# Turning q by DMA transposes of 16-bit halves instead of by TensorE, in a linear-attention and multiplicative-FFN kernel

## The chip, the cores and the metric

The kernel runs on one core of a Trainium2 chip. The metric is the time of one execution on the device, in microseconds; the time before is the median of three runs. The profile is one further execution of the same kernel, recorded by the hardware profiler.

The engines of the core are named as the profile names them: PE is TensorE (matmuls), PEld its weight loads, DVE is VectorE, ACT is ScalarE, POOL is GpSimd, and SP is SyncE, which issues most of the transfers. Each of them works through its own instructions in order, and waits for another engine where an instruction needs its result.

## What is computed

A linear attention without softmax, followed by a feed-forward part without a nonlinearity other than a product:

```python
# q, k, v: (8 batches, 8 heads, 576 tokens, 64), float32
kv  = np.einsum('bhsd,bhse->bhde', k, v)
out = np.einsum('bhsd,bhde->bhse', q, kv)
rms = np.sqrt(np.mean(out * out, axis=-1, keepdims=True) + 1e-06)
x   = out / rms * g_norm                      # then (B,H,S,D) -> (B*S, H*D): 4608 x 512
a   = x @ w1                                  # 512 -> 1024
b   = x @ w2                                  # 512 -> 1024
h   = a * b @ w3                              # 1024 -> 1024
return (h @ w_out).astype(np.float32)         # 1024 -> 512
```

The product of q with kv sums over the 64 dimensions of a head. A matmul on TensorE sums over partitions, so q must be turned: it comes from memory with tokens on the partitions, and the product wants dimensions on the partitions. This turning of q is what the change is about.

## The kernel before

The weights w3 and w_out are first multiplied together. Then the 4608 tokens are worked through in nine groups of 512: eight groups of the first 512 tokens of each batch, and one group of the eight batches' leftover 64 tokens each. All large matmuls use Strassen-Winograd's seven products. While the matmuls of a group run, the attention of the next batch is laid between them in eight pieces. The order on TensorE is as written; the order on the other engines is set by a scheduler outside the start-up.

One pair of heads of q (128 partitions x 512 words, 256 KB) is loaded into one of two buffers, turned by four transposes into a bank of PSUM, and copied to SBUF by ScalarE. The leftovers of two batches are turned together in the same way:

```python
def q_t(r):
    q_sb = loaded["q", b, r]
    qt_ps = bank(ps_at, "at").rearrange("p (e i t) -> p e i t", e=2, i=2)
    for e in range(2):
        for i in range(2):
            nc.tensor.transpose(qt_ps[:, e, i, :], q_sb[:, e, i * P:(i + 1) * P], ident)   # L297
    qT[r] = work.tile([P, 2, 2, P], FP32, name="qT")      # two buffers
    nc.scalar.copy(qT[r], qt_ps)                          # L299

def q_t_left():
    st["qT"] = work.tile([P, NP, P], FP32, name="qT_left", bufs=1)
    qt_ps = bank(ps_at, "at").rearrange("p (r t) -> p r t", r=NP)
    for r in range(NP):
        nc.tensor.transpose(qt_ps[:, r, :], q_left[b // 2][:, 2 * r:2 * r + 2, :], ident)  # L307
    nc.scalar.copy(st["qT"], qt_ps)                       # L308
```

The products that read the turned q, and the norm behind them:

```python
def product(h):                                           # heads of pairs 2h and 2h+1
    o_ps = [bank(ps_at, "at") for _ in range(2)]
    ...
        nc.tensor.matmul(o_ps[l][...], lhsT=qT[r][rows, e, i, tokens], rhs=kv_b[...], ...)  # L348
    return norm(o_ps, [...])     # squares (ScalarE), sums (VectorE), root (ScalarE), scale (VectorE)
```

How the attention is laid between the matmuls; piece n runs at the n-th call of `between`, which is called twice in each of the four Winograd blocks of a group:

```python
def begin_q(*rs):
    for r in rs:
        q_t(r)
        load_ahead("q", r)        # the load of the next q into the buffer that is now free

fs = [[] for _ in range(8)]
if b == 1:
    fs[0].append((a.begin_kv, 0, 1))
fs[0].append((a.begin_q, 0, 1))
fs[1] += [(a.begin_kv, 2, 3), (a.finish, 0)]              # finish(h): product(h) and its norm
fs[2].append((a.begin_q, 2, 3))
fs[3] += [(a.turn, 0), (a.turn, 1)]
if more:
    fs[5].append((batch(b + 1).begin_kv, 0, 1))
fs[5].append((a.finish, 1))
fs[7] += [(a.turn, 2), (a.turn, 3)]
if b % 2:
    fs[2].insert(0, (a.q_t_left,))
    fs[6].append((a.product_left,))
    fs[7].append((a.turn_left,))
    ...
```

One Winograd block, with the copies that ScalarE makes between the products. The matmul banks are a pool of five; a product into `r1` a second time adds to what stands in it, and so has to wait until ScalarE has copied it:

```python
def keep(name, ps):
    t = late_tile(name)...
    nc.scalar.copy(t, ps)                                 # L512
    return t

r1 = product("a11", "b11")                                # product: four matmuls, L499
p1 = keep("p1", r1)
r2 = product("s1", "t1")
p5 = keep("p5", r2)
product("s2", "t2", r1)
u2 = keep("u2", r1)
between()
product("s4", "b22", r2)
done("c12", r2, u2)
product("s3", "t3", r1)
u3 = keep("u3", r1)
done("c22", p5, u3)
r3 = product("a12", "b21")
done("c11", r3, p1)
between()
product("a22", "t4", r1)
done("c21", r1, None)                                     # copies half to c by ScalarE, L633
```

Of the kernel before, what the change touches and what calls it, by code (L numbers as in the profile page):

```python
# [10 lines left out]

FP32 = mybir.dt.float32
U32 = mybir.dt.uint32
I64 = mybir.dt.int64
AF = mybir.ActivationFunctionType
ALU = mybir.AluOpType
# [4 lines left out]
def kernel(  # L21
# [32 lines left out]
    nc = tc.nc  # L54
    PSUM = bass.MemoryType.PSUM
    P = 128
# [4 lines left out]
    NP = H // 2  # L61
# [11 lines left out]
    work = ctx.enter_context(tc.tile_pool(name="work", bufs=2))  # L73
    ps_mm = ctx.enter_context(tc.tile_pool(name="ps_mm", bufs=5, space=PSUM))
    ps_at = ctx.enter_context(tc.tile_pool(name="ps_at", bufs=3, space=PSUM))
# [5 lines left out]
    def bank(pool, tag):  # L81
        return pool.tile([P, 512], FP32, name=tag, tag=tag)


    loaded = {}
    q_left = {}
# [43 lines left out]
    def conversion(n, dst, raw, cols=slice(0, 1024)):  # L130

        dst, raw = (t if len(t.shape) == 3 else t[:, cols] for t in (dst, raw))
        if raw.dtype == FP32:
            yield
            nc.vector.tensor_copy(out=dst, in_=raw)
            return
        words = raw.bitcast(U32).rearrange("p (n w) -> p n w", w=2)
        lo, hi = words[:, :, 0], words[:, :, 1]

        low = ab[n % 2][:, NF // 2:].rearrange("p a i t -> p (a i t)")[:, cols]  # L140
        low_bits = low.bitcast(U32)
        if len(dst.shape) == 3:
# [96 lines left out]
    ident = const.tile([P, P], FP32, name="ident")  # L239
# [13 lines left out]
    def keep_warm(n):  # L253

        t = bank(ps_mm, "mm")
        for _ in range(n):
            nc.tensor.matmul(t[:, 0:P], lhsT=ident, rhs=ident, start=True, stop=True)


    def attention(b):  # L260
        kv_b = kv_sb[b % 3]
        qT = {}
# [35 lines left out]
            qT[r] = work.tile([P, 2, 2, P], FP32, name="qT")  # L298
            nc.scalar.copy(qT[r], qt_ps)  # L299

        st = {}

        def q_t_left():
            st["qT"] = work.tile([P, NP, P], FP32, name="qT_left", bufs=1)
            qt_ps = bank(ps_at, "at").rearrange("p (r t) -> p r t", r=NP)
            for r in range(NP):
                nc.tensor.transpose(qt_ps[:, r, :], q_left[b // 2][:, 2 * r:2 * r + 2, :], ident)  # L307
            nc.scalar.copy(st["qT"], qt_ps)  # L308

        def norm(o_ps, dsts):  # L310

# [98 lines left out]

        def begin_q(*rs):
            for r in rs:
                q_t(r)
                load_ahead("q", r)

        def begin(r):
            begin_kv(r)
            begin_q(r)

        def finish(h):  # L420
            all_of(product(h))

        return SimpleNamespace(**{f.__name__: f for f in (
            start, begin_kv, begin_q, begin, product, finish, turn, q_t_left, product_left, turn_left,
        )})

    batches = {}

    def batch(b):
        if b not in batches:  # L430
            batches[b] = attention(b)
        return batches[b]

    def steps(b):


        a = batch(b)
        a.start()
        more = b + 1 < B
        fs = [[] for _ in range(8)]  # L440
        if b == 1:
            fs[0].append((a.begin_kv, 0, 1))
        fs[0].append((a.begin_q, 0, 1))
        fs[1] += [(a.begin_kv, 2, 3), (a.finish, 0)]
        fs[2].append((a.begin_q, 2, 3))
        fs[3] += [(a.turn, 0), (a.turn, 1)]
        if more:
            fs[5].append((batch(b + 1).begin_kv, 0, 1))
        fs[5].append((a.finish, 1))
        fs[7] += [(a.turn, 2), (a.turn, 3)]  # L450
        if b % 2:
            fs[2].insert(0, (a.q_t_left,))
# [3 lines that stand above are left out]
                fs[7].append((load_q_left, b + 1))  # L456
        elif more:
            fs[0].append((load_q_left, b + 1))
        return iter([lambda s=s: [f(*args) for f, *args in s] for s in fs])
# [163 lines left out]
    def gates(T, p, between, ready=lambda name: None):  # L623
        def done(name, one, two):
            multiply(name, one, two)
            ready(name)

        def multiply(name, one, two):

            dst = ab[int(name[1]) - 1][:, p, int(name[2]) - 1, :]  # L630
            if two is None:
                c = late_pool.tile([P, N], FP32, name="c21")
                nc.scalar.copy(c, one[:, 0, :])  # L633
                nc.vector.tensor_mul(dst, c, one[:, 1, :])
# [245 lines left out]
    with tc.manual_schedule(  # L880
# [84 lines left out]
    groups = [*range(B - 1), B, B - 1]  # L965
    for n, T in enumerate(groups):
        pieces = steps(T + 1) if n + 2 < NG else iter([])

        def between():
            next(pieces, lambda: None)()  # L970

        for p in range(NF):
            if T and p + 1 == NF:
                sum_1, sum_2, sum_4, sum_3 = sum_ab(p)
                following = {
                    "c12": [], "c22": [sum_1],
                    "c11": [
                        lambda: sum_inner(0, lambda: all_of(f() for f in (sum_2, sum_3))),
                        lambda: sum_inner(1),
                    ],  # L980
                    "c21": [sum_4],
                }
                gates(T, p, between, lambda name: all_of(f() for f in following[name]))
                continue
            gates(T, p, between if T or p else lambda: None)
            if T == 0:
                if p + 1 < NF:
                    run(sum_w(p + 1))
                for _ in range(2):
                    if len(converted) < len(todo):  # L990
                        begin_next()
                        end_next()
                if p + 1 == NF:
                    allocate_projection()
                    run(*(f(i) for i in range(NF) for f in (sum_ab, combine_w3o)))
            else:
                run(sum_ab(p))
        last = n + 1 == NG
        if T:
            project_twice(T, last, [] if last else combine_x(groups[n + 1]))  # L1000
            continue
        project(T, between)
        run(combine_x(1))
        prepare_b()
        for _ in range(3):
            load_b()
        stage = stage_tile()
        inner_sums.append([stage[:, i] for i in range(3)])
# [30 lines left out]
```

## Time and profile before

| | |
|---|---|
| time, median of three runs | 794.01 us (793.12 to 795.03) |
| span of the profiled execution | 792.2 us |
| granted TensorE clock, mean | 0.999 of full speed |
| TensorE busy | 784.4 us, 99% |
| VectorE busy | 499.0 us, 63% |
| ScalarE busy | 282.2 us, 36% |
| DMA | 117.60 MB, mean 148 GB/s |
| transposes of q on TensorE | 128 of pairs (L297), 16 of leftovers (L307) |

A float32 matmul shows as two records, a transpose as one. The steady part of the kernel repeats every 79 to 80 us, once for each group of tokens: some 57 us of Winograd blocks with attention between them, then 22 us of the projection (L771). From 647 us on there is no attention left to lay between the matmuls. The first 100 us are the folding of w3 and w_out, the attention of batch 0 and the conversion of the weights; there, transfers are waited for.

### The profile page before, as it was taken

The page shows a single profiled execution, that of the slowest core. Times are in us where ns is not written, and L with a number is a line of the kernel's source. Part 1 is how long each engine was busy: PE and PEld are TensorE (multiplying, and loading weights), DVE is VectorE, ACT ScalarE, POOL GpSimd, SP SyncE. Part 2 cuts the span into 40 slices and gives each one's busy share as a digit, 9 for nine tenths or more (in the row PEclk, how much of TensorE's full clock was granted, in tenths as well). Part 3 has the DMA queues.
Part 4 walks back from the last instruction along what each step waited for, and adds up shares of the span by engine and source line. Part 5 has one row for each costly group of instructions (what it writes and reads, how often), then busy time and mean ns, then how long its engine had stood idle before and what let it go on. Part 6 is the DMA issues. An engine that isn't in the chain of part 4 may idle for free.

```text
span 792.2 us, 14634 instructions
## 1 busy us (share of the span) xinstructions
PE 784.4 (99%) x6003; PEld 683.1 (86%) x6003; DVE 499.0 (63%) x1050; ACT 282.2 (36%) x540; POOL 24.8 (3%) x36
## 2 busy tenths in 40 slices
PE   8999999999999999999999999999999999999998
PEld 5455788888899889988998899889988998899897
DVE  7968999425575558555755576457645765485366
ACT  6677643223332433233323332333233322222221
POOL 0010003410000000000000000000000000000000
PEclk9999999999999999999999999999999999999999
DMA  9996653574138412841284119411810180055015
GB/s 321 339 334 178 190 148 127 191 265 157 54 99 305 110 54 84 298 120 54 88 297 129 54 56 314 130 54 67 307 34 2 60 308 12 1 191 189 1 34 186
DMA packets 72582, 117.60 MB, mean 148 GB/s; under 512 B 16452, under 2 KB 60484, under 8 KB 72516
## 3 DMA queue, kind: packets, MB, share of 16 engines
q1 hardware_dynamic: 70064, 101.86, 40.2%
q10 hardware_dynamic: 2452, 14.81, 5.4%
q8 instruction: 47, 0.77, 0.4%
q14 instruction: 19, 0.16, 0.1%
HBM read 100.27 MB, written 16.38 MB: 147 GB/s over the span
## 4 chain that ended last, share of the span: by engine, by line
PE 96%; DMA 3%; ACT 1%; DVE 0%; SPq 0%; issue 0%; DVEq 0%; ACTq 0%
PE mm L499 58%; PE mm L771 22%; PE mm L481 6%; PE at L278 3%; PE at L348 2%; PE at L297 2%; PE at L381 2%; DMA raw<-in_moe_w_dram 2%; DMA raw<-in_moe_w_out_dram 1%; PE at L468 1%; PE mm L823 0%; PE at L366 0%; PE at L390 0%; PE at L307 0%; DVE inv L317 0%; ACT w_sb L149 0%
## 5 line engine op out<-in xcount | busy, mean ns | idle before, releaser
L499 PE MATMUL mm<-xT,w_sb 128*128 128x256 f32 x768 | 176.2, 379 | 0.0
L499 PEld LDWEIGHTS mm<-xT,w_sb 128*128 128x128 f32 x768 | 145.5, 190 | 20.0 <-issue 0.5
L499 PE MATMUL mm<-xc,ws 128*128 128x256 f32 x576 | 130.4, 379 | 0.0
L499 PEld LDWEIGHTS mm<-xc,ws 128*128 128x128 f32 x576 | 109.4, 190 | 15.2 <-ACT p L512 0.3
L637 DVE TENSOR_TENSOR c<-mm,u 128x512 f32<-128x512 f32 x36 | 24.9, 690 | 153.6 <-PE mm L499 153.4
L512 ACT COPY u<-mm 128x512 f32<-128x512 f32 x74 | 43.3, 585 | 146.5 <-PE mm L499 141.9
L512 ACT COPY p<-mm 128x512 f32<-128x512 f32 x74 | 43.3, 585 | 88.0 <-PE mm L499 85.5
L499 PE MATMUL mm<-xc,w_sb 128*128 128x256 f32 x288 | 69.6, 385 | 0.0
L771 PE MATMUL mm<-w3o_sb,raw 128*128 128x128 f32 x500 | 62.2, 275 | 0.0
L481 PE MATMUL mm<-chunks,ab 128*128 128x512 f32 x128 | 60.2, 601 | 1.6 <-ACT chunks L149 1.0
L499 PE MATMUL mm<-xT,ws 128*128 128x256 f32 x256 | 60.9, 381 | 0.4 <-ACT p L512 0.4
L771 PEld LDWEIGHTS mm<-w3o_sb,raw 128*128 128x128 f32 x500 | 59.0, 192 | 0.2
L499 PEld LDWEIGHTS mm<-xc,w_sb 128*128 128x128 f32 x288 | 52.5, 190 | 7.3 <-ACT u L512 0.3
L499 PEld LDWEIGHTS mm<-xT,ws 128*128 128x128 f32 x256 | 47.2, 190 | 6.7 <-ACT p L512 0.8
L638 DVE TENSOR_TENSOR ab<-c 128x256 f32<-128x256 f32 x108 | 46.7, 433 | 3.1
L637 DVE TENSOR_TENSOR c<-p,u 128x512 f32<-128x512 f32 x36 | 24.9, 691 | 35.5 <-ACT u L512 35.5
L771 PE MATMUL mm<-w3o_sb,ab 128*128 128x128 f32 x336 | 43.7, 275 | 0.0
L782 ACT COPY u<-mm 128x512 f32<-128x512 f32 x23 | 13.5, 585 | 83.9 <-DVE raw L795 43.4
L317 DVE TENSOR_REDUCE inv<-sq 128x8 f32<-128x512 f32 (+1 forms) x40 | 23.4, 627 | 31.6 <-ACT sq L316 31.6
L481 PEld LDWEIGHTS mm<-chunks,ab 128*128 128x128 f32 x128 | 21.9, 190 | 22.6 <-issue 15.8
L771 PEld LDWEIGHTS mm<-w3o_sb,ab 128*128 128x128 f32 x336 | 41.0, 192 | 0.3
L633 ACT COPY c<-mm 128x256 f32<-128x256 f32 x36 | 13.4, 372 | 48.4 <-PE mm L499 48.4
(150 smaller groups left out, 1109.9 us busy)
## 6 DMA issues: line engine op xcount, KB each, us to landing
w3o_sb<-w3o_l SPq DMA_DIRECT2D x26, 896.0 KB, 5.3
raw<-in_moe_w_dram SPq DMA_DIRECT2D x31, 512.0 KB, 7.4
raw<-w3o_l SPq DMA_DIRECT2D x13, 896.0 KB, 4.6
w3o_sb<-w3o_l ACTq DMA_DIRECT2D x11, 896.0 KB, 4.6
k_sb<-in_k_dram SPq DMA_DIRECT2D x32, 256.0 KB, 3.9
v_sb<-in_v_dram SPq DMA_DIRECT2D x32, 256.0 KB, 4.6
q_sb<-in_q_dram SPq DMA_DIRECT2D x32, 256.0 KB, 4.1
out_dram<-raw SPq DMA_DIRECT2D x14, 512.0 KB, 5.1
```

The source lines that it names most:

```text
L278: nc.tensor.matmul(kv_ps[e * D:(e + 1) * D, r - rs[0], :], lhsT=k_sb[:, e, cols] if j < J else kl[:, 2 * r + e, :], rhs=v_sb[:, e, cols] i ...
L297: nc.tensor.transpose(qt_ps[:, e, i, :], q_sb[:, e, i * P:(i + 1) * P], ident)
L317: nc.vector.tensor_reduce(out=inv[:, i], in_=sq.rearrange("p (h d) -> p h d", d=D), axis=AX.X, op=ALU.add)
L348: nc.tensor.matmul(o_ps[l][tokens, n * D:(n + 1) * D], lhsT=qT[r][rows, e, i, tokens], rhs=kv_b[rows, e, r, :], start=True, stop=True,)
L381: nc.tensor.transpose(t_ps[:, j, :], st[r // 2][:, j // 2, j % 2, m:m + 2, :], ident)
L481: nc.tensor.matmul(sums_ps[half][m], lhsT=w3T[half, c][:, m, :], rhs=chunks[:, c, 1, :], start=(c == 0), stop=(c == KF - 1),)
L499: nc.tensor.matmul(ps[:, u, :], lhsT=lhsT(a_name, u, c), rhs=rhs(b_name, c),  start=(u == 0 and c == 0 and to is None), stop=(c == chunks ...
L512: nc.scalar.copy(t, ps)
L637: nc.vector.tensor_add(c, one, two)
L638: nc.vector.tensor_mul(dst, c[:, 0, :], c[:, 1, :])
L771: nc.tensor.matmul(to[:, i, :], lhsT=x[:, c, :], rhs=y[:, c, :], start=new and place // 4 not in seen, stop=(c == 1), skip_group_check=True,)
L782: nc.scalar.copy(t[:, 0:4], ps[0])
```

## The change

Instead of transposing q on TensorE, the kernel uses the transpose that a DMA can do while it moves data within SBUF. [...] each float32 is taken as two 16-bit halves. ScalarE first copies q so that all first halves stand together and all second halves behind them (into the buffer that will hold the result); one DMA transposes all eight 128 x 128 blocks of halves back into the buffer of q; ScalarE puts the halves together again. The bits are not changed. Its purpose is to take the transposes of q off TensorE.

Batch 0, whose attention lies in the start-up, keeps the transposes on TensorE. Because the way by DMA is longer, pairs 0 and 1 of a batch are begun earlier: in piece 6 of the batch before, or, for batch 1, at the first piece of the first group.

```diff
+    def turn_by_dma(dst, src):
+        def words(t):
+            return t.bitcast(U16).rearrange("p (n w) -> p n w", w=2)
+        def planes(t):
+            return t.bitcast(U16).rearrange("p (w n) -> p w n", w=2)
+
+        nc.scalar.copy(planes(dst).rearrange("p w n -> p n w"), words(src))       # "split"
+        nc.sync.dma_start_transpose(
+            out=src.bitcast(U16).rearrange("p (a t) -> p a t", t=P), in_=dst.bitcast(U16)
+        )
+        nc.scalar.copy(words(dst), planes(src).rearrange("p w n -> p n w"))       # "merge"
 ...
+        def q_by_dma(r):
+            qT[r] = work.tile([P, 2, 2, P], FP32, name="qT")
+            turn_by_dma(
+                qT[r].rearrange("p e i t -> p (e i t)"), loaded["q", b, r].rearrange("p e n -> p (e n)")
+            )
 ...
         def q_t_left():
             st["qT"] = work.tile([P, NP, P], FP32, name="qT_left", bufs=1)
-            qt_ps = bank(ps_at, "at").rearrange("p (r t) -> p r t", r=NP)
-            for r in range(NP):
-                nc.tensor.transpose(qt_ps[:, r, :], q_left[b // 2][:, 2 * r:2 * r + 2, :], ident)
-            nc.scalar.copy(st["qT"], qt_ps)
+            turn_by_dma(
+                st["qT"].rearrange("p r t -> p (r t)"), q_left[b // 2].rearrange("p h d -> p (h d)")
+            )
 ...
         def begin_q(*rs):
             for r in rs:
-                q_t(r)
+                q_by_dma(r)
                 load_ahead("q", r)
 
         def begin(r):                      # batch 0 only
             begin_kv(r)
-            begin_q(r)
+            q_t(r)
+            load_ahead("q", r)
 ...
+        def begin_first():
+            if not first_done:
+                first_done.append(begin_q(0, 1))
 ...
-        fs[0].append((a.begin_q, 0, 1))
         fs[1] += [(a.begin_kv, 2, 3), (a.finish, 0)]
         fs[2].append((a.begin_q, 2, 3))
 ...
         fs[5].append((a.finish, 1))
+        if more:
+            fs[6].append((batch(b + 1).begin_q, 0, 1))
 ...
-            gates(T, p, between if T or p else lambda: None)
+            gates(T, p, between if T or p else lambda: batch(1).begin_first())
```

More of the change, by code (lines that the diff above doesn't have):

```diff
@@ L13 @@
 U32 = mybir.dt.uint32
+U16 = mybir.dt.uint16
 I64 = mybir.dt.int64
@@ L417, in begin @@
             begin_kv(r)
-            begin_q(r)
+            q_t(r)
+            load_ahead("q", r)
+        first_done = []
+        def begin_first():
+            if not first_done:
+                first_done.append(begin_q(0, 1))
         def finish(h):
@@ L423, in attention @@
         return SimpleNamespace(**{f.__name__: f for f in (
-            start, begin_kv, begin_q, begin, product, finish, turn, q_t_left, product_left, turn_left,
+            start, begin_kv, begin_q, begin_first, begin, product, finish, turn, q_t_left, product_left, turn_left,
         )})
```

## The prediction

> **What bounds the kernel now.** I read four views, in this order. First the page's busy times with the wait table of TensorE, to see which engine sets the end and whether it ever waits:
>
> ```profile
> PE 784.4 (99%) x6003; PEld 683.1 (86%) x6003; DVE 499.0 (63%) x1050; ACT 282.2 (36%) x540; POOL 24.8 (3%) x36
> ```
>
> ```profile
> PE mm L257 <- POOL ident masks.py:199: 2.0, 1, 2.0
> PE mm L481 <- ACT chunks L149: 1.0, 1, 1.0
> PE mm L481 <- ACT ab L473: 0.6, 1, 0.6
> PE mm L499 <- ACT p L512: 0.4, 1, 0.4
> ```
>
> TensorE is busy 99% of the span, and its own wait table (line waited for: us in total, times, longest) holds 4.0 us in all, half of it at the very start. So an instruction taken off TensorE shortens the span by what it takes there. The reader should not take busy time for that: matmul records overlap. The chain that ended last, in order of time, gives it without the overlap:
>
> ```profile
> 263.81 5.61 PE mm L499 x26
> 269.42 0.44 PE at L307 x4
> 269.86 0.87 PE at L297 x8
> 270.73 4.32 PE mm L499 x20
> ```
>
> Twelve transposes hold the chain for 0.44 + 0.87 = 1.31 us, or 0.109 us each, and the matmuls stand flush on both sides. The group table gives "17.2 us, 128 records" for L297, 0.134 us each; I use the chain.
>
> Third, ScalarE, because the change moves work there. It is 36% busy, but what counts is how late it may be. The timeline of a steady stage (one group of 512 tokens, 329 to 408 us):
>
> ```profile
> 346.45 3.62 PE L499 MATMUL mm<-xc,ws 128*128 128x256 f32 x16
> 346.65 0.58 ACT L512 COPY p<-mm 128x512 f32<-128x512 f32 x1 [1.15 <-PE mm L499]
> ...
> 348.37 0.58 ACT L512 COPY p<-mm 128x512 f32<-128x512 f32 x1 [1.14 <-PE mm L499]
> ...
> 349.90 1.04 PE L297 MATMUL at<-ident,q_sb 128*128 128x128 f32 x8
> 350.15 0.59 ACT L512 COPY u<-mm 128x512 f32<-128x512 f32 x1 [1.20 <-PE mm L499]
> ...
> 350.64 1.08 ACT L299 COPY qT<-at 128x512 f32<-128x512 f32 x2
> ```
>
> A Winograd product is 8 matmul records, 1.73 us. It is copied out of its bank while the next product runs, and the product after that accumulates into the same bank. So a copy of 0.58 us has 1.73 us less a start of about 0.2 us: ScalarE may be late by **about 0.95 us** before TensorE waits. The "1.15" idle time before each copy is the same margin seen from the other side. This is the number the case turns on.
>
> Fourth, the DMA issues: how long a transfer of this size takes to land.
>
> ```profile
> k_sb<-in_k_dram SPq DMA_DIRECT2D x32, 256.0 KB, 3.9
> ...
> q_sb<-in_q_dram SPq DMA_DIRECT2D x32, 256.0 KB, 4.1
> ...
> out_dram<-raw SPq DMA_DIRECT2D x3, 256.0 KB, 2.2
> ```
>
> **What the Trainium skill says.** "TensorE: Matmul & The Clock Gate", Part 4: PE-mode transpose, gives about 275 ns for a transpose in a kernel's context; the trace has 272 to 273 ns per record, but records overlap and each costs the engine 109 ns, so taking 275 would promise 35 us in place of 14. "ScalarE: Activation LUTs", What ACT_TABLE_LOAD costs, gives 0.833 ns per element beside a fixed part; the trace agrees (585 ns at 512 and 372 ns at 256 elements: 0.832 ns each). "VectorE: DVE Perf Modes", The three transpose paths, gives 1309 ns for one 128x128 transpose of 2-byte values by DMA. "DMA: Bandwidth & Descriptors", Latency and other measured facts, gives 261 GB/s for DMA transposes whose middle dimension is not contiguous. No transpose by DMA is in this trace, so the last two are estimates' raw material only.
>
> **The change part by part.** *Removed from TensorE.* Batches 1 to 7 lose 16 transposes each (112), and four leftovers of q lose 4 each (16). Batch 0 keeps its own. In the chain these are fourteen pieces of L297 after 100 us, thirteen of 0.87 and one of 1.03 us, and four of L307 at 0.44 us: 11.31 + 1.03 + 1.76 = **14.1 us**. That is the whole possible gain, 1.8% of 794.0, so a gain of over 2% is nearly excluded.
>
> *Moved on ScalarE.* Each of 32 turns (28 pairs of heads, 4 leftovers) loses one copy of 0.60 us (32 x 0.60 = 19 us) and gets two of 1024 16-bit elements, one that takes the halves apart and one that puts them together. 0.832 x 1024 and the fixed 0.16 us of the PSUM copies make 1.01 us; the conversions of 1024 elements out of SBUF (L149) took 1.17 us. I take 1.1 us: 64 x 1.1 = 70 us, net +51 us, ScalarE from 282 to about 333 us, 42%. No bound by itself.
>
> *Added on DMA.* 32 transposes of 256 KB within SBUF, 8.4 MB beside 117.6 MB. Bytes are no issue; the landing time is. Estimates: 256 KB at the skill's 261 GB/s is 1.0 us on top of the 2.2 us that a 256 KB store took here: 3.2 us at best. Eight blocks at 1309 ns one after another would be 10.5 us. I choose **4.0 us**, near the low end, since 16 engines should share the blocks, plus some waiting behind loads on the same queue.
>
> *The new wait.* ScalarE works in order. In the built kernel the order on ScalarE around the second product of a batch is
>
> ```
> split q2; squares x2; split q3; copy c; sqrt; copy p1; copy p5; merge q2; merge q3; copy u2
> ```
>
> and around the next batch's pairs
>
> ```
> split q0; squares x2; split q1; sqrt; copy c; merge q0; copy p1; merge q1; copy p5; copy u2
> ```
>
> A merge stands at the head of ScalarE until its transpose has landed, and the copies behind it free TensorE's banks. I lay these on the stage shown above.
>
> Group A (pairs 2, 3): the first product of the attention ends at about 342.9; split q2 343.0 to 344.1, squares to 345.2, split q3 to 346.3. SyncE issues loads of k and v until 345.1, so the first transpose lands at 345.1 + 4.0 = 349.1 and the second at about 350.6. Merges 349.1 to 350.2 and 350.6 to 351.7, then u2 to 352.3. With its transposes gone TensorE wants that bank at 349.90 + 1.73 = 351.6. Stall 0.7 us, seven times: 4.9 us.
>
> Group B (pairs 0, 1 of the next batch): split q0 ends at 372.65, its transpose lands at 376.65, merge to 377.75, p1 to 378.35, wanted at 376.7: stall 1.65 us. Merge q1 waits until 378.85, p5 is done at 380.55, wanted at 380.1 in batches without a leftover product: 0.45 us in half of them. 1.9 us on average, six times: 11.4 us.
>
> Leftovers: split and merge have one or two instructions between them, so ScalarE stands still for most of the landing time, at a place where the copies wanted next are a little later; I put 1.2 us on each of four, 4.8 us. The first group (batch 1, pairs 0, 1) lies in the start-up, where transfers are waited for anyway: 0.5 us.
>
> Sum: 794.0 - 14.1 + 4.9 + 11.4 + 4.8 + 0.5 = **801.5 us**.
>
> **The rivals.** *R1, the transfer is hidden.* If a transpose lands within about 3 us, group A fits in the margin, B loses a few tenths, and nearly all of the 14.1 us remains: 780 to 786 us. For it: the product that needs the turned q comes some 19 us after the split (269.9 to 288.8 in the stage before), DMA is busy 42% of the stage, ScalarE has idle time between all copies. Against it: the merges stand early in ScalarE's order, not just ahead of their use. *R2, the transpose is slow.* Every microsecond of landing beyond 4 is paid about 18 times (7 + 6 + 1 groups + 4 leftovers), since ScalarE's margin is spent by then. 6 us gives about 838 us; 10 us would give some 910. For it: 16-bit pieces, and the 1309 ns for one block. Against: the 261 GB/s. *R3, ScalarE becomes the bound by its work alone.* Two merges back to back are 2.2 us against a margin of 0.95; that would cost up to 1.2 us in each group A even at no landing time, but they follow a copy that has just been served, and the next one is not due for another 1.2 us. I give it under 5 us in all. *R4, SyncE's queue.* Loads of q now wait for merges, and loads of k and v stand behind them. Loads are issued a whole stage ahead, so I expect nothing from it outside the first 110 us.
>
> **How range and chances follow.** Landing times from 2.7 to 6 us span 782 to 838 us, and 4.0 lies at 801.5; break-even is near 3.5 us. Over 2% faster means under 778.1, below even a change with no cost (779.9): 0.03. Over 2% slower means over 809.9, a landing time of about 4.5 us: somewhat less likely than not, 0.37. The rest, 0.60, is within 2%.
>
> **What would show it.** Right: no L297 after 100 us on TensorE; ScalarE copies of 16-bit halves at 1.0 to 1.2 us, x64, busy about 333 us; transposes in the DMA issues landing in about 4 us; in the wait table of TensorE new lines of waits for ScalarE's p and u, about 20 us in all, and for ScalarE waits of merges on DMA. Wrong if those waits are near zero (R1), or far over 30 us (R2); also if the wait stands at the product that reads the turned q, which I expect never to wait, or at matmuls that want w or k and v (R4).

## The result, and the profile after

The changed kernel takes **918.17 us** (916.92 to 919.58), against 793.71 us for the kernel before (793.12 to 795.03): a ratio of **1.1566, 95% interval 1.1539 to 1.1593**. The prediction was 801.5 us with a range of 782 to 838. The direction of its sum was right, the size was not.

First the page's line of busy times:

```profile
PE 810.4 (89%) x5875; PEld 693.3 (76%) x5875; DVE 499.5 (55%) x1050; ACT 442.1 (48%) x572; POOL 27.5 (3%) x36
```

TensorE has 128 instructions fewer, as intended, and yet is busy 26 us longer. ScalarE is busy 442 us where the prediction had put 333. The groups of instructions say which of its instructions took the time (busy us, mean ns of one, idle time before and what ended it):

```profile
L270 ACT COPY qT<-q_sb 128x1024 uint16<-128x1024 uint16 x28 | 132.2, 4721 | 1.3 <-PE at L371 1.0
L274 ACT COPY qT<-q_sb 128x1024 uint16<-128x1024 uint16 x28 | 32.7, 1167 | 17.6 <-DMA q_sb<-qT 17.6
```

L270 is the split and L274 the merge. Both copy 1024 halves on 128 partitions. The merge takes 1.17 us, close to the 1.1 us that I took for both; **the split takes 4.72 us**. Nothing waits inside it: idle time before it is 1.3 us in all. The transfer between the two lands sooner than the 4.0 us that I chose (the DMA issues, median us from issue to landing):

```profile
q_sb<-qT SPq DMA_TRANSPOSE x28, 3.1
```

What a slow split does to TensorE stands in TensorE's wait table (us in total, times, longest):

```profile
PE mm L530 <- ACT p L543: 85.6, 13, 8.6
```

The wait is of the kind that the prediction described, a matmul that wants its bank back from ScalarE's copy of p, but thirteen times for 6.6 us on average. One of the thirteen, on the timeline of ScalarE (start, duration, what; in brackets the idle time before it):

```profile
405.29 4.74 ACT L270 COPY qT<-q_sb 128x1024 uint16<-128x1024 uint16 x1
410.05 1.09 ACT L339 ACTIVATE sq<-at 128x512 f32<-128x512 f32 x2
411.02 4.70 ACT L270 COPY qT<-q_sb 128x1024 uint16<-128x1024 uint16 x1
...
415.37 0.57 ACT L664 COPY c<-mm 128x256 f32<-128x256 f32 x1
415.83 1.08 ACT L543 COPY p<-mm 128x512 f32<-128x512 f32 x2
416.78 1.19 ACT L274 COPY qT<-q_sb 128x1024 uint16<-128x1024 uint16 x1
418.86 1.16 ACT L274 COPY qT<-q_sb 128x1024 uint16<-128x1024 uint16 x1 [0.89 <-DMA q_sb<-qT]
```

and the same moment on the timeline of TensorE:

```profile
406.99 1.89 PE L530 MATMUL mm<-xT,w_sb 128*128 128x256 f32 x8
408.71 1.89 PE L530 MATMUL mm<-xc,ws 128*128 128x256 f32 x8
416.48 3.78 PE L530 MATMUL mm<-xc,ws 128*128 128x256 f32 x8 [5.88 <-ACT p L543]
```

This is the order that the prediction had read from the built kernel (only the root and copy c have changed places): split, squares, split, root, copy c, copy p. The two splits fill 405.3 to 415.7. The product that ends near 408.9 is copied out only at 415.8. TensorE makes one more product, is done with it at 410.6, wants the first one's bank back, and stands for 5.88 us. The transfer is not what it waits for: the first merge comes behind that copy and finds its data there.

The last line shows one thing more. The eight records after the wait take 3.78 us, the eight before it 1.89 us. Three windows: before the end of that wait, after it, and the one that follows (length; busy time of PE, PEld, DVE, ACT, POOL with the number of instructions; granted TensorE clock; DMA share; GB/s):

```profile
410.00:416.40 6.40, 0.60 (x3) 0.19 (x1) 1.80 (x4) 6.38 (x8) 0.00 (x0) 0.93 0.24 44
416.40:422.40 6.00, 5.92 (x14) 4.76 (x15) 1.77 (x4) 3.32 (x5) 0.00 (x0) 0.51 0.53 131
422.40:426.40 4.00, 4.00 (x20) 3.46 (x20) 2.04 (x4) 0.59 (x1) 0.00 (x0) 1.00 0.00 0
```

**For some 6 us after the wait the granted clock is half of full speed**; over the whole span its mean is 0.938, against 0.999 before. The Trainium skill, "TensorE: Matmul & The Clock Gate", Part 1: The HAM clock gate, says that TensorE falls to half rate after an idle window of about 3.4 us and needs such a time of work to come back. The trace agrees in this case: half speed after 5.88 us. That a shorter wait can be enough is seen in e1 below. The prediction did not reckon with a lower clock; the longest of its single waits was 1.65 us.

The span of the profile can now be put together from TensorE alone. 14.1 us of transposes are gone. The wait table sums to 100.1 us instead of 4.0: +96.1. The thirteen waits on p are 85.6 of them; another 9.4 us are two waits in the start-up, where TensorE is to turn x (L404) and three splits of 4.7 to 4.9 us stand on ScalarE ahead of what it needs. Busy time is 810.4 us where 784.4 - 14.1 = 770.3 was due: +40.1. Most of this is the clock: 71.3 us of the busy time lie in stretches granted 0.50, and half of that, 35.6 us, would have been saved at full speed. -14.1 + 96.1 + 40.1 = 122.1 us; the span grew from 792.2 to 914.7, by 122.5.

A second account, by place, serves for all the experiments. The first TensorE instruction of each projection divides the span into the time up to the first projection, five groups of tokens from there to the start of the sixth, and the rest, in which there is hardly any attention left:

| kernel | to the first projection | five groups | rest | span |
|---|---|---|---|---|
| before | 226.6 | 398.5 | 167.1 | 792.2 |
| after | 272.0 | 475.5 | 167.2 | 914.7 |
| e1: split by plane | 242.1 | 409.7 | 167.2 | 819.0 |
| e2: slow split, no transfer | 272.8 | 487.7 | 167.1 | 927.6 |
| e3: split by plane, no transfer | 226.6 | 398.4 | 167.2 | 792.2 |
| e5: halves on GpSimd | 229.3 | 388.4 | 167.2 | 784.9 |
| e6: halves on VectorE | 233.2 | 390.8 | 167.1 | 791.1 |
| e7: e1, a store moved | 240.7 | 411.7 | 167.3 | 819.6 |
| e8: transposes left out | 222.4 | 388.5 | 167.9 | 778.8 |
| e9: GpSimd, batch 1 on TensorE | 224.0 | 388.4 | 167.3 | 779.7 |
| e10: e1, merges later, fixed order | 227.7 | 388.4 | 167.9 | 784.0 |

Of the 122.5 us, 45.4 were lost up to the first projection and 77.0 in the five groups.

### The profile page after: what moved, and what is told of

Read it like the earlier page. It is cut to its first block, busy times and chain, and to the rows that moved or that the text cites. A ratio compares the mean times of both kernels' runs of the same rounds, so it can differ in the third digit from the quotient of the medians.

```text
span 914.7 us, 14474 instructions
## 1 busy us (share of the span) xinstructions
PE 810.4 (89%) x5875; PEld 693.3 (76%) x5875; DVE 499.5 (55%) x1050; ACT 442.1 (48%) x572; POOL 27.5 (3%) x36
## 4 chain that ended last, share of the span: by engine, by line
PE 76%; ACT 16%; issue 3%; DMA 3%; DVE 1%; POOL 1%; SPq 0%; DVEq 0%; POOLq 0%; ACTq 0%
PE mm L530 45%; PE mm L802 18%; ACT qT L270 10%; PE mm L512 6%; PE at L295 2%; PE at L371 2%; ACT sq L339 2%; ACT qT_left L270 2%; PE at L404 1%; DMA raw<-in_moe_w_out_dram 1%; ACT qT L274 1%; ACT p L543 1%; DMA raw<-w3o_l 1%; ACT inv L344 1%; PE at L499 1%
## 5 line engine op out<-in xcount | busy, mean ns | idle before, releaser
L530 PE MATMUL mm<-xc,ws 128*128 128x256 f32 x576 | 154.9, 425 | 77.0 <-ACT p L543 77.0
L530 PEld LDWEIGHTS mm<-xc,ws 128*128 128x128 f32 x576 | 121.5, 213 | 100.7 <-ACT p L543 81.8
L270 ACT COPY qT<-q_sb 128x1024 uint16<-128x1024 uint16 x28 | 132.2, 4721 | 1.3 <-PE at L371 1.0
L530 PE MATMUL mm<-xT,ws 128*128 128x256 f32 x256 | 69.6, 420 | 0.0
L530 PEld LDWEIGHTS mm<-xT,ws 128*128 128x128 f32 x256 | 56.1, 221 | 10.4
L813 ACT COPY u<-mm 128x512 f32<-128x512 f32 x23 | 13.5, 586 | 84.4 <-DVE raw L826 43.4
L802 PEld LDWEIGHTS mm<-w3o_sb,ab 128*128 128x128 f32 x336 | 41.2, 192 | 0.9 <-DVE ab L669 0.6
L274 ACT COPY qT<-q_sb 128x1024 uint16<-128x1024 uint16 x28 | 32.7, 1167 | 17.6 <-DMA q_sb<-qT 17.6
```

The source lines that it names most:

```text
L270: nc.scalar.copy(planes(dst).rearrange("p w n -> p n w"), words(src))
L274: nc.scalar.copy(words(dst), planes(src).rearrange("p w n -> p n w"))
L530: nc.tensor.matmul(ps[:, u, :], lhsT=lhsT(a_name, u, c), rhs=rhs(b_name, c),  start=(u == 0 and c == 0 and to is None), stop=(c == chunks ...
L802: nc.tensor.matmul(to[:, i, :], lhsT=x[:, c, :], rhs=y[:, c, :], start=new and place // 4 not in seen, stop=(c == 1), skip_group_check=True,)
```

## The experiments

Spans are those of the profiled execution; times are medians on the device, and every ratio is against the kernel before on the same chip.

### e1: the same split, written plane by plane

The split of the changed kernel walks through q in order and writes each word's two halves in turn to two places, half a buffer apart. Here the loops are exchanged: all first halves are written in one run, then all second halves. What is read, written and computed is the same, and so is the order of instructions on ScalarE.

```diff
-        nc.scalar.copy(planes(dst).rearrange("p w n -> p n w"), words(src))
+        nc.scalar.copy(planes(dst), words(src).rearrange("p n w -> p w n"))
```

> The split walks its 1024 halves plane by plane instead of word by word: it writes two runs of 512 neighbours and reads every second half, and nothing else changes, not even the order on ScalarE. Theory S (ScalarE pays for 2-byte writes that jump between two far places, 4.6 ns each): the split falls from 4.72 us to 1.0 to 1.2 us, TensorE's waits for p copies from 85.6 us to under 30, and the time to 790 to 815 us. Rival D (the landing of the transposes holds ScalarE): the split may get faster, but ScalarE then waits for the landing by as much more; time above 870. Rival R (16-bit elements at a stride are slow on either side): the split stays near 4.7 us and the time near 918.

Measured: **821.67 us** (819.23 to 823.09), ratio 1.0341 (1.0315 to 1.0368). The split takes 1.05 us, ScalarE is busy 330.3 us. One exchanged pair of loops takes 96.5 us off the changed kernel. So nearly four fifths of the loss was the order in which the split writes. The time is above the 790 to 815 us expected, still 28 us slower than before. The wait tables of ScalarE and of TensorE show what is left:

```profile
ACT qT L274 <- DMA q_sb<-qT: 32.0, 15, 10.7
...
PE mm L530 <- ACT p L543: 20.8, 7, 9.6
...
PE mm L530 <- ACT u L543: 8.4, 6, 2.1
```

Now merges do stand at the head of ScalarE until their transfer has landed, and TensorE waits 29.2 us in all on p and u (e3 shows that a part of this needs no transfer). The longest wait of a merge, 10.7 us, lies in the start-up. ScalarE's timeline there:

```profile
155.19 1.16 ACT L274 COPY qT<-q_sb 128x1024 uint16<-128x1024 uint16 x1 [10.74 <-DMA q_sb<-qT]
```

and that of SyncE, which issues the transfers:

```profile
141.95 5.32 SPq L729 DMA_DIRECT2D w3o_l<-stage  x2
...
149.53 1.23 SPq L271 DMA_TRANSPOSE q_sb<-qT  x1
...
152.51 2.78 SPq L271 DMA_TRANSPOSE q_sb<-qT  x1
```

The split of that pair was done at 141.9, but its transpose was issued at 149.5: SyncE was held at two stores of folded weights (L729), whose data GpSimd was still making, and then issued four loads. Against the kernel before, the table puts 15.5 us of the loss ahead of the first projection and 11.2 in the five groups.

Two of TensorE's waits in e1 also say something of the clock:

```profile
313.58 3.68 PE L530 MATMUL mm<-xc,ws 128*128 128x256 f32 x8 [2.14 <-ACT p L543]
...
563.89 1.99 PE L530 MATMUL mm<-xc,ws 128*128 128x256 f32 x8 [2.09 <-ACT p L543]
```

After nearly the same wait the same eight records take 3.68 us in one place and 1.99 in the other. Of the six waits of 2.0 to 2.2 us in e1, three were followed by 3.4 us at a granted clock of 0.50 and three by none. So a wait shorter than the 3.4 us quoted above can be followed by half the clock, and here the measurement decides; what makes the difference was not followed up.

### e2: the slow split kept, the transfer left out

The split as in the changed kernel, no DMA transpose, and a merge that copies q as it stands. This kernel leaves the turning out: the products read q unturned.

```diff
-        nc.sync.dma_start_transpose(...)
-        nc.scalar.copy(words(dst), planes(src).rearrange("p w n -> p n w"))
+        nc.scalar.copy(words(dst), words(src))
```

> The slow split stays, the DMA transposes are left out: the merge copies q as it is, so the products read an unturned q. Theory S: only the waits for landing go, 17.6 + 6.8 us in ScalarE's table, and what stood behind SyncE's queue; time 885 to 905 us. Rival D: without transposes nothing is waited for; time below 820 us.

Measured: **930.43 us** (929.3 to 932.95), ratio 1.1718 (1.1691 to 1.1745), slower than with the transfers and above the 885 to 905 us expected. Up to the first projection it needs what the changed kernel needs (272.8 and 272.0 us). The loss of 122 us thus does not need the transfers: while the split is slow, they land behind splits. That it is even 12 us slower in the five groups fits the order on ScalarE, where merges with nothing to wait for now stand close behind their splits, so that one or two copies of 1.04 us more lie in front of the copy of p; TensorE waits 102.1 us for p instead of 85.6.

### e3: split by plane, the transfer left out

Both edits together; the products again read q unturned.

> Split by plane, and no transposes (the products read an unturned q): what the two copies on ScalarE cost by themselves at these places. Theory S: copies of 1.1 us fit into ScalarE's gaps, time 779 to 788 us, at most 8 us above 779.9, which is 794.0 less the 14.1 us taken off TensorE. Rival (ScalarE's work alone is too much): above 800 us. The difference to the run with split by plane and transposes is the price of landing and of SyncE's queue: 5 to 25 us.

Measured: **794.63 us** (793.69 to 796.19), ratio 1.0008 (0.9999 to 1.0017). No transfer, a fast split, and still nothing is gained, where 779 to 788 us had been expected: the 14.1 us come back somewhere else. The table shows the five groups as long as before the change (398.4 and 398.5). The chain that ended last, in order of time, shows where:

```profile
290.20 1.04 ACT qT L270
...
291.26 1.04 ACT qT L271
...
292.33 1.09 ACT sq L336 x2
293.42 0.27 ACT c L661
293.68 0.94 ACT qT L270
294.62 0.21 ACT inv L341
294.83 0.93 ACT qT L271
295.76 0.50 ACT p L540
```

For 6 us the chain runs over ScalarE (L270 split, L271 the copy in place of the merge). Splits, copies, squares, c and root stand in a row, each after the other, with the copy of p last. TensorE waits for it 0.8 us, and it does so twelve times, as its wait table says:

```profile
PE mm L527 <- ACT p L540: 9.6, 12, 0.8
```

What the prediction gave "under 5 us in all" as rival R3 is the whole gain, 13.9 us when compared with e8 below; 9.6 us of it are these waits.

### e4: the disputed copies by themselves

The kernel before, with nine copies added on free buffers whose results nothing reads. It was run once, for the time of each copy alone.

```diff
+        nc.scalar.copy(d, s16)                                                    # flat
+        nc.scalar.copy(planes(d).rearrange("p w n -> p n w"), words(s16))         # the split as changed
+        nc.scalar.copy(planes(d), words(s16).rearrange("p n w -> p w n"))         # plane by plane
+        nc.scalar.copy(words(d)[:, :, 0], s16[:, 0:512])                          # every second half only
 ...                                          # 256 and 512 float32 with gaps; three copies on VectorE
```

> The kernel before, with nine copies of one 128 x 512 float32 tile added ahead of the last group, each in another access pattern, to measure the disputed cost by itself. ScalarE, 16-bit: flat 1.17 us; word by word into two planes (as in the change) 4.7 us; plane by plane 1.17 us. 512 halves written with gaps of 2 bytes: 0.74 us if only far jumps cost, 2.4 us if any 2-byte write without a neighbour costs. 4-byte elements: 256 written with gaps 0.53 us; 512 alternating between two far places 0.74 us if only 2-byte writes suffer, 2.4 us if the jump itself costs. VectorE, 16-bit: word by word, plane by plane, and merge, each 1.1 us if VectorE has no such cost, 4 to 5 us for the first if it has.

The groups of instructions; flat, the split as changed, and every second half (the copy by plane took 1.34 us here, 1.05 us in e1):

```profile
L444 ACT COPY sq<-qT 128x1024 uint16<-128x1024 uint16 x1 | 1.0, 1045 | 0.2 <-DVE inv L318 0.2
...
L446 ACT COPY sq<-qT 128x1024 uint16<-128x1024 uint16 x1 | 4.7, 4747 | 0.0
...
L450 ACT COPY sq<-qT 128x512 uint16<-128x512 uint16 x1 | 0.8, 782 | 0.0
```

The split costs 4.75 us with nothing beside it, so it is the instruction and no collision. Gaps alone do not do it: 512 halves with a gap of two bytes between them took 0.78 us. Nor does jumping between two distant places: 512 float32 words written to two places in turn took 1.13 us (0.62 us in order, in e8). It needs halves and jumps together. VectorE has the same weakness in a milder form: 2.76 us for the split as changed, 0.69 us by plane, 0.69 us for the merge.

### e8: the transposes left out, nothing put in their place

The kernel before with its 128 transposes taken out and one copy of ScalarE from SBUF in place of the copy from PSUM; the products read q unturned. This measures what the removal alone is worth.

```diff
-            qt_ps = bank(ps_at, "at")...
-            for e in range(2):
-                for i in range(2):
-                    nc.tensor.transpose(qt_ps[:, e, i, :], ...)
-            nc.scalar.copy(qT[r], qt_ps)
+            if b:                                             # batch 0 keeps its transposes
+                nc.scalar.copy(qT[r], q_sb.rearrange("p e (i t) -> p e i t", i=2))
```

> The kernel before without the transposes of q on TensorE for batches 1 to 7 and the leftovers, and with nothing in their place but one ScalarE copy of q as it is (so the products read an unturned q): what the removal itself is worth. By the chain 14.1 us: 780 us, within 2. Rival (the transposes filled time that TensorE would wait anyway, since the run without DMA transposes came out at 794.6): 788 to 794 us.

Measured: **780.72 us** (779.98 to 781.28), ratio 0.9827 (0.9813 to 0.9842), 13.4 us less. The prediction's 14.1 us from the chain was right within 5%. No version below came under it, and I call it the floor.

### e5 and e6: the halves handled by another engine

The splits (by plane) and merges go to GpSimd in e5 and to VectorE in e6; the transfers stay.

```diff
-        nc.scalar.copy(planes(dst).rearrange("p w n -> p n w"), words(src))
+        nc.gpsimd.tensor_copy(out=planes(dst), in_=words(src).rearrange("p n w -> p w n"))
 ...
-        nc.scalar.copy(words(dst), planes(src).rearrange("p w n -> p n w"))
+        nc.gpsimd.tensor_copy(out=words(dst), in_=planes(src).rearrange("p w n -> p n w"))
```

(nc.vector.tensor_copy in e6.)

> Split by plane, and both split and merge on GpSimd, which is 3% busy and on which no bank of TensorE waits; the transposes stay. If what is left of the loss (821.7 us with split by plane) is ScalarE standing at its two copies and at the landing, it goes away: TensorE's waits for p and u under 5 us, time 779 to 788 us, better than both kernels. Rival: GpSimd slows VectorE beside it, or is itself too slow (over 4 us for a copy of 1024 halves), and the product waits for the turned q: 795 to 830 us.

> Split by plane, and both on VectorE, where the probe gave 0.69 us for each form in place of 1.05 and 1.16 us on ScalarE. VectorE is 63% busy and also empties banks; it now stands at the landing in ScalarE's place. If the waiting in order is what costs, the loss is about as with ScalarE: 795 to 815 us. If only the length of the copies costs, 780 to 790 us.

Measured: e5 **786.90 us** (785.97 to 788.86), ratio 0.9909 (0.9892 to 0.9926); e6 **791.88 us** (790.54 to 793.85), ratio 0.997 (0.9955 to 0.9986).

In e5 the five groups take 388.4 us, the floor of e8: over the whole kernel GpSimd stands 67 us in front of the pairs' merges waiting for transfers to land, and nobody needs it meanwhile. The same landing times that cost e1 11 us or more on ScalarE cost nothing here. What e5 loses it loses up to the first projection (229.3 against 222.4 us). There VectorE is busy in every microsecond of the window from 90 to 125 us, in e8 as in e5, and its instructions grow longer while GpSimd copies. The timeline of GpSimd:

```profile
119.87 2.71 POOL L274 COPY qT<-q_sb 128x1024 uint16<-128x1024 uint16 x2 [4.33 <-DMA q_sb<-qT]
```

and that of VectorE during it and after it:

```profile
121.49 1.63 DVE L583 TENSOR_TENSOR w_sb<-w_sb 128x512 f32<-128x512 f32 x1
123.05 0.68 DVE L583 TENSOR_TENSOR ws<-w_sb,ws 128x512 f32<-128x512 f32 x1
```

1.63 us beside GpSimd, 0.68 us without it; in e8 the first of the two took 0.69 us as well. The Trainium skill, "GPSIMD Engine Reference", 1. Specifications, says that GpSimd shares its SBUF interfaces with VectorE and contends with VectorE's instructions of two SBUF inputs; the trace agrees in that, and GpSimd suffers too: its merges take 1.15 us as a rule and up to 5.24 us there (beside that longest one, VectorE's conversions took as long as in e8). That this makes up e5's loss is not shown by itself.

In e6 VectorE now has the waits for landing, 41.2 us on 23 merges, and some of its own work stands behind them; it loses 10.8 us against e8 up to the first projection and 2.3 in the five groups. Its time lies in neither of the two ranges expected.

### e7: one store taken off SyncE's queue

e1, with the stores that held SyncE (L729) issued by GpSimd, which makes their data.

```diff
-            nc.sync.dma_start(
+            nc.gpsimd.dma_start(
                 out=w3o_l2[n, :, 1024:PART], in_=stage.rearrange("p i c n -> p (i c n)")
             )
```

> Split by plane on ScalarE as before; only the seven stores of sums that GpSimd makes (w3o_l from stage, in the first group) are issued by GpSimd instead of SyncE, so that the transposes of batch 2 no longer stand behind them in SyncE's queue. If that queue made the single wait of 9.6 us (merge at 144 to 155 us), the time falls by 8 to 11 us from 821.7, to 811 to 814 us. Rival (the transposes were late for another reason): 818 us or more.

Measured: **817.64 us**, but scattered from 811.4 to 823.2; ratio 1.0274 (1.0203 to 1.0345), an interval that overlaps that of e1. In the profiled execution, one of 821 us, the wait of 10.7 us had become 5.2, and a leftover's merge then waited 13.9 us: its transpose was issued 6.7 us after its split, behind other stores of the same queue (L726). The wait moved on to the next transfer in line. The time lies between the two ranges expected. As a test of how much of the start-up is SyncE's queue, this is inconclusive; why the runs scatter was not followed up.

### e10: the merges later, on ScalarE

e1, with each merge (and the load that follows it) taken out of begin_q and put two pieces later, close to the product that reads it, and with ScalarE's order kept as written instead of left to the scheduler.

```diff
+        fs[0].append((a.end_q, 0, 1))        # merges of pairs 0 and 1, begun in piece 6 of the batch before
 ...
         fs[2].append((a.begin_q, 2, 3))
         fs[3] += [(a.turn, 0), (a.turn, 1)]
+        fs[4].append((a.end_q, 2, 3))
 ...
-    ctx.enter_context(tc.manual_schedule(engines={mybir.EngineType.PE}))
+    ctx.enter_context(tc.manual_schedule(engines={mybir.EngineType.PE, mybir.EngineType.Activation}))
```

> Split and merge stay on ScalarE, by plane, with the transposes; but ScalarE follows the written order, and the merges are written two pieces after the splits (pairs 2 and 3: split in piece 2, merge in piece 4; pairs 0 and 1: split in piece 6, merge in piece 0 of the next batch), so that both copies of a group stand behind a copy u2 that has just been served. Theory (what is left of the loss with split by plane is ScalarE's order: copies heaped behind the product, and merges that wait for landing): TensorE's waits for p and u under 8 us, time 781 to 792 us. Rival (ScalarE's added work or the transposes cost it wherever they stand): 795 to 815 us.

Measured: **787.50 us** (786.47 to 788.53), ratio 0.9916 (0.9902 to 0.9929). ScalarE does the same work as in e1 (329.9 and 330.3 us busy) and the five groups take 388.4 us, the floor. So ScalarE is not too slow for this work; the 21 us that e1 lost to e8 in these five groups came from where the work stood. What is lost lies up to the first projection (227.7 against 222.4), and TensorE's wait table has one new line of over 1 us:

```profile
PE mm L540 <- ACT p L553: 4.5, 2, 2.9
```

The two edits (later merges, written order) were not tried apart.

### e9: GpSimd, with the start-up left to TensorE

e5, but batch 1's pairs and the first leftovers, whose turning falls into the time when VectorE is full, keep their 20 transposes on TensorE (and pairs 0 and 1 of batch 1 their old place).

```diff
             for r in rs:
-                q_by_dma(r)
+                (q_t if b == 1 else q_by_dma)(r)
                 load_ahead("q", r)
```

(and q_t_left in the same way for batch 1.)

> Split and merge on GpSimd, by plane, but batch 1 and the first leftovers keep TensorE's transposes, since its turns fall into the start-up where VectorE is fully busy and was slowed beside GpSimd (683 in place of 427 ns for the small products). Theory: the 6.9 us that GpSimd's kernel loses before the first projection against the kernel without any turning go away, for 20 more transposes, 2.2 us: 782 to 784 us. Rival (the loss at the start has another cause, such as the queue of SyncE): 786 us or more.

Measured: **782.10 us** (780.98 to 782.72), ratio **0.9846** (0.9833 to 0.986). It removes 108 transposes, 11.8 us at 0.109 us each, and gains 12.0. TensorE's wait table sums to 3.1 us. This is the best version that computes everything, 1.4 us above the floor of e8. Since the transfers of batch 1 go along with its copies on GpSimd, the run does not tell which of the two had cost e5 its time in the start-up.

### e11 and e12: what makes the halves slow

Again the kernel before with added copies, each run once. e11 writes 1024 halves in runs of 2, 4, 8, 16 and 32 before each jump, brings the two places close together (32 bytes apart), and puts the split as changed on GpSimd. e12 writes halves one at a time into 4, 8, 16 and 32 places in turn, and 512 halves to two places so that each has a word of its own and no word is written twice.

```diff
+        nc.scalar.copy(runs(d, 2), s16.rearrange("p (c w n) -> p c w n", w=2, n=2))          # e11
 ...
+        nc.scalar.copy(d.rearrange("p (w n) -> p n w", w=32), s16.rearrange("p (n w) -> p n w", w=32))   # e12
 ...
+        nc.scalar.copy(d.rearrange("p (w n t) -> p n w t", w=2, t=2)[:, :, :, 0],            # e12, own words
+                       s16[:, 0:512].rearrange("p (n w) -> p n w", w=2))
```

> Added copies ahead of the last group again: the same 1024 halves written by ScalarE into two planes, in runs of 2, 4, 8, 16 and 32 neighbours between the jumps; then word by word into planes only 32 bytes apart (blocks of 16); then word by word into far planes on GpSimd. If each jump costs about 3.6 us / 1024 = 3.5 ns: runs of 2 take 2.9 us, of 4 2.0, of 8 1.5, of 16 1.3, of 32 1.2 us. If only the distance matters, the near planes take about 1.1 us; if any break in a run of neighbours costs, 4.7 us. GpSimd: 1 to 3 us if it has no such cost.

> Added copies ahead of the last group, all by ScalarE: 1024 halves written in turn into 4, 8, 16 and 32 places instead of two; then 512 halves in turn into two far places where each 4-byte word gets one half only; then 512 float32 in turn into 32 places. Theory W (a half is slow when it completes a 4-byte word whose other half was written one or two writes before): with more places the word is met again later, and the copy gets faster, down to about 1.1 us at 32; the halves that complete no word take under 1.2 us. Theory J (every half written away from its neighbour costs 4.6 ns): 4.7 us at every number of places, and 2.5 us for the 512 halves. The float32 copy: 1.1 us if jumping costs 1 ns each as with two places, 0.6 us if not.

The groups of instructions of e11, runs of two:

```profile
L447 ACT COPY sq<-qT 128x1024 uint16<-128x1024 uint16 x1 | 1.1, 1096 | 0.2 <-DVE inv L318 0.2
```

and of e12, 32 places in turn and halves in words of their own:

```profile
L456 ACT COPY sq<-qT 128x1024 uint16<-128x1024 uint16 x1 | 4.7, 4736 | 0.0
...
L460 ACT COPY sq<-qT 128x512 uint16<-128x512 uint16 x1 | 2.8, 2789 | 0.0
```

Two neighbours together are enough: runs of 2 to 32 took 1.03 to 1.10 us. One half at a time is slow wherever it goes: two places 32 bytes apart 4.88 us, 4 to 32 places 4.74 to 5.05 us, and on GpSimd 4.77 us. That words are written a second time later is not the cause, since 512 halves in words of their own took 2.79 us, 5.1 ns for each half. 512 float32 words into 32 places took 1.05 us. So the price goes with every half written away from the one before it, about (4740 - 190) / 1024 = 4.4 ns beyond the fixed part, where 190 ns is what flat 1024 halves leave after 0.832 ns each. One observation of e4 limits what "away" means: 512 halves at a constant step of four bytes took 0.78 us, not 2.8. In every slow form each half lies some 30 bytes or more from the one before it; distances between 4 and 30 bytes were not tried. What the hardware does inside stays open.

## Why the prediction was wrong, step by step

**The gain, 14.1 us: right.** e8 measured 13.4. Taking the cost from the chain instead of from the mean of the records was the right choice.

**The step that failed: "I take 1.1 us: 64 x 1.1 = 70 us, net +51 us, ScalarE from 282 to about 333 us".** The working took two copies for one kind, because they have the same number of elements of the same type. It drew their price from copies of float32 that wrote in order, 0.832 ns per element beside a fixed part. That holds for the merge (1.17 us) and for the split by plane (1.05 us in e1); it says nothing of a copy that writes single halves in turn to two places. That this one does so stood in the diff: `planes(dst).rearrange("p w n -> p n w")` on the side that is written. Measured, the term is 28 x 4.72 + 4 x 4.78 + 32 x 1.17 = 188.7 us, not 70.

**The margin, 0.95 us: right, and that is why the error was so dear.** 3.6 us more for a split, twice in each of two places per group, is nearly all beyond the margin, and paid by TensorE. In the place shown above, the copy of p would have begun near 409.0 us and began at 415.83, 6.8 us late; TensorE waited 5.88 us, so about 0.9 us cost nothing. In 13 places TensorE waited 6.6 us on average for p.

**The clock: not in the sum at all.** Some 36 of the 122 us are matmuls at half clock behind those waits.

**The landing time, 4.0 us: not what failed.** Transposes landed in 3.1 us (median), and in e1 in 4.5. So in the changed kernel the sum had its sign right by luck: what made it positive, merges that wait for landing, is not what TensorE waited for. R2, the slow transfer, gave "some 910"; the figure came near by luck as well, as e2 shows: without any transfer the time is 930.

**With the split at the price I had assumed, what remains of the sum?** e1 is that kernel, and it took 821.7 us where I had said 801.5. My waits were 21.6 us in all. Before the first projection lie five of the fourteen turns of two pairs and two of the four leftovers: 0.5 + 2 x 0.7 + 2 x 1.9 + 2 x 1.2 = 8.1 us; the other 13.5 fall into the five groups. Against e8, e1 lost 19.7 us before the first projection and 21.2 in the five groups, so both places were too small, by 11.6 and by 7.7 us. e3, which has no transfers, tells the two causes apart, if one takes them as a sum: it lost 4.2 and 9.9 us to e8 in the same two places, by the work on ScalarE and its order alone (R3); the transfers add 15.5 and 11.3. In the five groups the waits for landing, which my 13.5 us were for, were thus about right (11.3), and what was missing is R3. The waits also stood where I had put them: in these groups 1.0 to 2.1 us on u in group A, where I had 0.7, and 2.0 to 2.1 us on p in group B, where I had 1.65. Ahead of the first projection, "Loads are issued a whole stage ahead, so I expect nothing from it outside the first 110 us" (R4) is the sentence that failed: from 142 to 147 us SyncE stood at stores whose data was still being made, with transposes behind them. How much of the 15.5 us is this queue is not settled, since e7 was inconclusive.

**R3, "under 5 us in all": too small by 9.** e3 has neither slow splits nor transfers and loses 13.9 us to e8, of which 9.6 us are TensorE's waits behind splits, copies and squares standing in a row ahead of a copy of p; the rest was not followed. I had looked at two merges in a row; the row was eight long.

**R1, the hidden transfer:** its 780 to 786 us were there to be had, though not in this order on ScalarE. e9 (782.1) is in that range, and e5 and e10 (786.9 and 787.5) are just above it.

**Right besides:** the product that reads the turned q did not wait in the steady groups, and the new waits stood on p (in e1 on p and u).

## What to carry to other kernels

Price a copy by its access pattern as well as by its elements, on the written side above all: if values of 16 bits must be scattered, exchange the loops so that each run that is written is at least two neighbours long (1.10 us in runs of two, 1.05 us in the runs of 512 of e1, instead of 4.72). An engine at 36% may still have only a microsecond of margin at the places where others wait for it; work that waits for a transfer belongs on an engine for which nobody waits, or close ahead of its use, not at the head of the engine that frees the matmul banks. To know what a removal is worth before its replacement is tuned, leave the work out and time that (e8): it set the 13.4 us that the removal gains apart from the 124 us that the change lost on balance.

## What the runs showed of the hardware that I had not expected

- Halves of 32-bit words, written one at a time away from each other: 4.7 to 5.0 us for 1024 on 128 partitions on ScalarE, 4.8 on GpSimd, 2.8 on VectorE; in runs of two or more 1.0 to 1.1 us on ScalarE. At a constant step of four bytes it was not so: 512 halves took 0.78 us. Reading them that way costs little: the merge took 1.17 us on ScalarE and 0.69 on VectorE.
- A DMA transpose of eight 128 x 128 blocks of halves within SBUF landed in 3.1 us (median), far below the 10.5 us that the prediction had estimated for blocks one after another; it held SyncE for 1.24 us at issue (median).
- After a wait of 5.9 us TensorE's granted clock was 0.50 for the next 5.8 us, so that a wait cost more than its length: over the kernel some 36 us on top of 96. Waits of 2.0 to 2.2 us were followed by 3.4 us at 0.50 in three of six cases in e1.
- GpSimd and VectorE were slower in places where both worked on SBUF: VectorE's 0.68 us became 1.63, GpSimd's 1.15 up to 5.24.
